# Scores of two pairs of heads per turn of TensorE, and products with v in two parts

## The chip, the cores and the metric

One NeuronCore of a Trainium2 chip runs the whole program in one launch. The metric is the device time of one execution in microseconds (us). The engines are TensorE (PE, with its weight loads as PEld), VectorE (DVE), ScalarE (ACT), GpSimd (POOL) and SyncE (SP, which mostly issues DMAs).

## The reference

Talking-heads attention over 4 batches, 12 heads, 448 positions and 64 columns, then two feed-forward parts. Only the attention is touched by the change:

```python
scores = scale * np.matmul(q, k.transpose(0, 1, 3, 2))
scores = np.einsum('bhij,hg->bgij', scores, w_pre)       # heads mixed before the softmax
scores = scores - np.max(scores, axis=-1, keepdims=True)
attn = np.exp(scores)
attn = attn / (np.sum(attn, axis=-1, keepdims=True) + 1e-09)
attn = np.einsum('bhij,hg->bgij', attn, w_post)          # and after it
x = np.matmul(attn, v)                                   # [4, 12, 448, 64] -> [1792, 768]
```

Behind it stand `h = x @ w_in; x = (h * cos(h)) @ w_out` and a soft mixture of 8 experts with `phi`, `w1` and `w2`. All data are float32; `w_in` and `w_out` come as 64-bit floats and are narrowed by the kernel.

## The kernel before

The program has three stages. `phase_a` is the attention, `phase_b` the first feed-forward part, `phase_c` the experts. `phase_b` begins when the attention ends (`start_b` is called by `phase_a` as `start_next` ahead of its last products), and reads `xT_d`, which the attention writes to DRAM.

`phase_a` works on 16 query tiles (4 for each batch, of 120 rows, or 90 in the short one), and on 60 groups of 30 mixed rows within them (4 groups a tile, 3 in the short one). For a tile:

- `q_prep` (L310) turns q by TensorE (tile `qt`) and splits it into two parts, `q_hi` and `q_lo`. `k_prep` (L287) does the same for k once a batch (`kt`, six of them).
- `scores` (L347) multiplies one pair of heads at a time: six matmuls, three for each head, on 64 rows of the array each, the two heads side by side in the upper and lower half (tiles `s`; such a run is called a score episode). Two copies take the results out of PSUM to `ss` (ACT or DVE), and a DMA from POOL sorts each head into `s2`, so that heads stand beside rows.
- `pre` (L395): for each group three matmuls with the mixing matrix (`pre`), a maximum on DVE (`mz`, L409), an exponential on ACT (`e`, L413). `fin` (L423) makes the group's weights `wc` on DVE.
- `post` (L437): four results for each group (`po`, three matmuls each), copied to `am`.
- `av` (L486): the products with v, in three parts of four heads. Each head uses 64 columns of the array (tiles `av`, L468); a copy takes each part to `xst`, and a DMA stores the tile.

Beside this, 64 pieces of `w_in` and `w_out` are narrowed (`narrow`, L506) on DVE, ACT and POOL.

None of this is issued as it is written. Each step is an `Op` with the engines that may do it and an assumed duration, with what it depends on, the buffers it takes and a due time in units of groups. `Plan.schedule` (L115) goes through time with these durations, takes for each engine the op that can start first and is due earliest, and so writes one fixed order for every engine. A change between ops marked `half` (scores and products) and all others adds `TURN` to an op, and `STAY` to its due time. Due times follow from constants: scores of a tile are due `S_DUE` groups ahead of its first group, spread over `S_SPAN`; k is turned `K_DUE` ahead of its scores; a group's `pre` is due `P_DUE` ahead, the products `AV_DUE` behind a tile's last group, spread over `AV_SPAN`.

PSUM has eight banks: three for `pre`, two for `po`, three (`ps`) for `s`, `kt`, `qt` and `av`. The first 24 users of `ps` take turns over all eight by the list `SPARE`. SBUF has eight `ss` buffers, two `s2`, one `xst`.

Of the kernel before, what the change touches and what calls it, by code (L numbers as in the profile page):

```python
# [56 lines left out]
class Slot:  # L57


    def __init__(self, tag):  # L60
        self.tag, self.users = tag, []


class Op:


    def __init__(self, ways, emit, deps, due, takes, moves, behind, half, late):
        self.ways, self.emit, self.due, self.half, self.late = ways, emit, due, half, late
        self.deps, self.takes, self.moves, self.behind = list(deps), list(takes), moves, list(behind)
        self.end = None  # L70


class Plan:
# [10 lines left out]
    def op(self, ways, emit, deps=(), due=0.0, takes=(), uses=(), moves=0.0, behind=(), half=False, late=0.0):  # L84


        o = Op(ways, emit, deps, due, takes, moves, behind, half, late)
# [27 lines left out]
    def schedule(self):  # L115
# [3 lines left out]
        after, halves = {}, False  # L119
# [4 lines left out]
        while ready:  # L124
            best = None
            starts = []
            for o in ready:
                r = self.room(o.takes)
                if r is None:
                    continue  # L130
                for e, dur in o.ways:
                    t = max([free[e], r] + [d.seen + (self.HOP if d.eng != e else 0.0) for d in o.deps]
                            + [d.start for d in o.behind])
                    if e == "PE" and o.half != halves:
                        dur += self.TURN
                    starts.append((t, t + dur, o, e, dur))
# [7 lines left out]
            for x in starts:  # L144
                t, end, o, e, dur = x
                if t <= first[e] + 0.05:
                    due = o.due + (STAY if e == "PE" and o.half != halves else 0.0)
                    if e not in pick or due < pick[e][0]:
                        pick[e] = (due, x)
# [10 lines left out]
            if e == "PE":  # L160
                halves = o.half
# [18 lines left out]
def phase_a(tc, ident, q, k, v, w_pre, w_post, xT_d, wide, start_next):  # L180
# [8 lines left out]
    with ExitStack() as ctx:  # L189
# [157 lines left out]
        def scores(ti, p, due):  # L347

            b, t = tiles[ti]
            n = ROWS[t]  # L350
            s = [Slot("ps") for _ in range(2)]
            x = {}

            def mul(e):
                pts = made["s", ti, p] = [bank(s[o], f"s{ti}_{2 * p + o}") for o in range(2)]
                for i, (x, y) in enumerate(((qh, kp), (qh, kr), (ql, kp))):
                    for o in range(2):
                        r = slice(64 * o, 64 * o + 64)
                        nc.tensor.matmul(pts[o][:n, :S], x[r, p, :n], y[r, p, :],  # L359
                                         start=(i == 0), stop=(i == 2))  # L360

            def out(o):
                def f(e):
                    if ti:
                        x[o] = room(sg, "ssrc", [120, S], F32, f"ss{ti}_{2 * p + o}")
                    else:

                        c = S * (2 * p + o)
                        x[o] = am[1].rearrange("p h t i -> p (h t i)")[:, c:c + S]
                    copy(e, x[o][:n], made["s", ti, p][o][:n, :S])  # L370
                return f

            def sort(o):
                h = 2 * p + o

                def f(e):
                    if h == 0:
                        s2t[ti] = room(sg, "s2", [120, 12, S], F32, f"s2_{ti}")
                    QUEUE[e].dma_start(out=s2t[ti][h::12, :n // 10], in_=x[o][:n])  # L379
                return f  # L380
            qk[ti, p] = plan.op([("PE", 0.8)], mul, [kdone[b, p], qdone[ti, p // 2]], due, takes=s, half=True)
            for o in range(2):
                h = 2 * p + o
                ss = [Slot("ssrc")] if ti else []
                if h == 0:
                    s2l[ti] = Slot("s2")
                c = plan.op(EV, out(o), [qk[ti, p]], due, takes=ss, uses=[s[o]])
                sorted_[ti, h] = plan.op([("POOL", 0.62)] if ti else [("SP", 1.0), ("POOL", 0.8)], sort(o), [c], due,
                                         takes=[] if h else [s2l[ti]], uses=ss + ([s2l[ti]] if h else []),
                                         moves=1.0 * n / 120, behind=[sorted_[ti, 0]] if h else [])  # L390
# [46 lines left out]
        def post(gi, jt, f, due):  # L437
# [10 lines left out]
            def out(e):  # L448
# [4 lines left out]
                                     [m] + ([avs[ti - 2, s] for s in range(3)] if ti > 1 else [sorted_[0, h] for h in range(H)] if ti else []), due, uses=[b])  # L453


        xst, xl = {}, {}

        def av_mul(ti, s, pt):
# [5 lines left out]
            for x in range(2):  # L464
                for jt in range(NJ):
                    for o in range(2):
                        g = 4 * s + 2 * x + o
                        nc.tensor.matmul(pt[64 * o:64 * o + 64, x * 120:x * 120 + n], vt[:, g, jt, :],  # L468
                                         am[ti % 2][:, g, jt, :n], start=(jt == 0), stop=(jt == NJ - 1))

        def av_out(ti, s, by):
            n = 30 * NG[tiles[ti][1]]
            copy(by, xst[ti][:, 2 * s:2 * s + 2, :n],
                 made["av", ti, s][:, :240].rearrange("p (x i) -> p x i", i=120)[:, :, :n])
# [11 lines left out]
        def av(ti, due):  # L486
# [4 lines left out]
            for s in range(3):  # L491
                d, sl_ = due + s / 3 * AV_SPAN, Slot("ps")
                avs[ti, s] = plan.op([("PE", 1.64)],
                                     lambda e, s=s, sl_=sl_: av_mul(ti, s, bank(sl_, f"av{ti}_{s}")),
                                     need + [vload[b, s]], d, takes=[sl_] + ([] if s else [xl[ti]]),
                                     uses=[xl[ti]] if s else [], behind=[avs[ti, 0]] if s else [], half=True)
                outs.append(plan.op([("ACT", 0.28), ("DVE", 0.36)], lambda e, s=s: av_out(ti, s, e),
# [59 lines left out]
        for b in range(B):  # L557
            for ti in range(4 * b, 4 * b + 4):
                g0, n = first[ti], NG[tiles[ti][1]]
                mark = [qk[ti - 1, 0]] if ti > 2 else [qk[1, 5]] if ti > 1 else [qk[0, 2]] if ti else []  # L560
                for p in range(6):
# [11 lines left out]
                    scores(ti, p, d)  # L573
# [19 lines left out]
        for s in range(3):  # L593
# [3 lines left out]
            av_out(NT - 1, s, "DVE" if s == 1 else "ACT")  # L597
# [669 lines left out]
```

## Time and profile before

| what | us |
|---|---|
| median of 3 runs (lowest, highest) | 911.07 (908.5, 912.84) |
| the profiled execution | 906.24 |
| its span, first to last instruction | 904.4 |
| TensorE busy in the span | 860.0 (95%) |
| VectorE, ScalarE, GpSimd busy | 627.5, 513.8, 178.9 |
| first matmul of `phase_b` | 498.24 |

A row of the trace has an instruction's start and length in us. Matmuls are pipelined, so that rows that follow each other overlap; what an instruction costs the engine is the distance from its start to the next start. A row with a count holds several equal instructions. A float32 matmul that isn't split by the kernel leaves two records (`po` x6 is one result of three matmuls, `pre` x2 one matmul, `av` x32 sixteen). Idle time stands behind a row in brackets with what ended it.

### The profile page before, as it was taken

Reading aid. Unit: us, or ns where it says so; the run is one execution under the profiler, and the core shown is the slowest. Engines: PE = TensorE matmul, PEld = TensorE weight load, DVE = VectorE, ACT = ScalarE, POOL = GpSimd, SP = SyncE. Lnnn points to the kernel's source line nnn. Section 1 sums busy time; section 2 is a strip of 40 time slices with the busy share of each in tenths; the row PEclk is TensorE's granted clock in tenths of the full one; section 3 lists DMA queues with packets and bytes.
Section 4 is the critical chain, followed back from the end, with each engine's and each line's share of the span. In section 5 each row is a group of like instructions: output and inputs, shape, how many; then the busy total and the mean of one; then the engine's idle time right before and its main releaser. Section 6 shows DMA issues by size and latency. Waiting matters only on the chain.

```text
span 904.4 us, 17763 instructions
## 1 busy us (share of the span) xinstructions
PE 860.0 (95%) x6636; PEld 605.2 (67%) x6636; DVE 627.5 (69%) x1286; ACT 513.8 (57%) x1134; POOL 178.9 (20%) x272
## 2 busy tenths in 40 slices
PE   7899999999999999999999799999999999989765
PEld 5467777776777777777778577776777787843212
DVE  4478878778779788788754687877877778843003
ACT  4477777677767777767655344555546457612003
POOL 2233443333434334334310000000000000010000
PEclk9999999999999999999999999999999999999778
DMA  7999897999788997979518892363464348899998
GB/s 166 202 197 232 221 241 207 221 209 270 215 211 223 237 233 174 253 211 236 155 32 225 224 212 73 120 215 135 158 226 141 122 153 273 298 339 411 418 401 307
DMA packets 181793, 198.91 MB, mean 220 GB/s; under 512 B 73600, under 2 KB 155458, under 8 KB 181708
## 3 DMA queue, kind: packets, MB, share of 16 engines
q1 hardware_dynamic: 164824, 159.18, 60.2%
q0 software_dynamic: 14272, 37.96, 18.7%
q8 instruction: 52, 0.85, 0.4%
q10 hardware_dynamic: 2612, 0.65, 0.4%
q14 instruction: 33, 0.27, 0.1%
HBM read 135.40 MB, written 23.59 MB: 176 GB/s over the span
## 4 chain that ended last, share of the span: by engine, by line
PE 83%; DMA 9%; DVE 2%; SPq 2%; ACT 2%; issue 1%; POOL 0%; DVEq 0%; ACTq 0%; POOLq 0%
PE po L444 17%; PE pre L406 15%; PE h L698 9%; PE av L468 8%; PE h L699 8%; PE h L701 8%; PE s L359 8%; DMA knat<-in_k_dram 2%; DMA ring<-in_moe_w_dram 2%; PE p L810 2%; DMA cg<-in_moe_w_dram 2%; PE eh L1061 2%; PE lg L749 1%; DMA s<-ss 1%; SPq L968 1%
## 5 line engine op out<-in xcount | busy, mean ns | idle before, releaser
L444 PEld LDWEIGHTS po<-wc,e 120*112 120x112 f32 x1440 | 171.6, 178 | 56.8 <-issue 42.5
L444 PE MATMUL po<-wc,e 120*112 120x120 f32 x1440 | 183.8, 270 | 0.5 <-ACT am L229 0.5
L406 PE MATMUL pre<-s,kron_pre 120*120 120x448 f32 x360 | 166.3, 551 | 3.8 <-ACT e L413 3.8
L379 POOL DMA_DIRECT2D s<-ss x180 | 107.0, 596 | 173.9 <-ACT ss L229 124.4
L409 DVE TENSOR_REDUCE mz<-pre 120x1 f32<-120x448 f32 x180 | 111.1, 621 | 42.4 <-PE pre L406 41.1
L698 PE MATMUL h<-x,wh 128*128 128x512 f32 (+1 forms) x384 | 140.0, 374 | 0.1
L699 PE MATMUL h<-x,wh 128*128 128x512 f32 (+1 forms) x384 | 136.6, 365 | 0.0
L413 ACT ACTIVATE e<-pre,mz 120x448 f32<-120x448 f32 x180 | 114.7, 638 | 25.2 <-DVE mz L409 22.7
L229 ACT COPY am<-po 112x360 f32<-112x360 f32 x190 | 87.6, 462 | 66.2 <-PE po L444 64.2
L698 PEld LDWEIGHTS h<-x,wh 128*128 128x128 f32 x384 | 72.4, 188 | 28.4 <-ACT cg L712 11.7
L701 PE MATMUL h<-x,wf 128*128 128x512 f32 (+1 forms) x384 | 87.7, 364 | 0.0
L712 ACT ACTIVATE cg<-h 128x512 int32<-128x512 f32 (+1 forms) x64 | 34.7, 541 | 90.8 <-PE h L701 88.3
L543 POOL TENSOR_TENSOR nar<-nar,cvt 128x384 uint32<-128x384 uint32 x64 | 64.2, 1003 | 98.4 <-DVE cvt L534 43.7
L468 PE MATMUL av<-am,v 112*64 112x120 f32 (+1 forms) x1536 | 83.0, 262 | 0.0
L468 PEld LDWEIGHTS av<-am,v 112*64 112x64 f32 x1536 | 74.0, 137 | 10.4 <-issue 5.5
L699 PEld LDWEIGHTS h<-x,wh 128*128 128x128 f32 x384 | 72.5, 189 | 11.3
L701 PEld LDWEIGHTS h<-x,wf 128*128 128x128 f32 x384 | 66.5, 188 | 11.9
L713 DVE SCALAR_TENSOR_TENSOR cg<-h,cg 128x512 f32<-128x512 f32 (+1 forms) x64 | 39.8, 622 | 48.4 <-ACT cg L712 48.4
L229 ACT COPY ss<-s 120x448 f32<-120x448 f32 (+1 forms) x104 | 54.1, 533 | 27.6 <-PE s L359 15.4
L1035 POOL MEMSET own<- 128x192 f32 x2 | 0.4, 253 | 345.3 <-PE si L1021 345.3
L651 DVE TENSOR_TENSOR wf<-wf,wh 128x768 fp32r<-128x768 f32 x64 | 60.9, 951 | 8.7 <-ACT wh L650 8.7
L406 PEld LDWEIGHTS pre<-s,kron_pre 120*120 120x120 f32 x360 | 53.2, 184 | 20.4 <-issue 11.7
(171 smaller groups left out, 1204.5 us busy)
## 6 DMA issues: line engine op xcount, KB each, us to landing
s<-ss POOLq DMA_DIRECT2D x144, 210.0 KB, 7.9
early<-in_moe_w_dram SPq DMA_DIRECT2D x36, 768.0 KB
wf<-w SPq DMA_DIRECT2D x64, 384.0 KB
raw<-in_moe_w_in_dram SPq DMA_DIRECT2D x32, 384.0 KB
w<-nar SPq DMA_DIRECT2D x64, 192.0 KB
raw<-in_moe_w_out_dram SPq DMA_DIRECT2D x32, 384.0 KB
gn<-in_moe_w_dram SPq DMA_DIRECT2D x16, 768.0 KB
early<-w SPq DMA_DIRECT2D x16, 384.0 KB
```

Source lines behind the costliest of these rows:

```text
L229: nc.scalar.copy(out=out, in_=in_)
L359: nc.tensor.matmul(pts[o][:n, :S], x[r, p, :n], y[r, p, :], start=(i == 0), stop=(i == 2))
L379: QUEUE[e].dma_start(out=s2t[ti][h::12, :n // 10], in_=x[o][:n])
L406: nc.tensor.matmul(prt[gi, c][:, :S], kpre, s2t[ti][:, 3 * g + c, :], start=True, stop=True)
L409: nc.vector.tensor_reduce(out=mz[gi][:, 0, c:c + 1], in_=prt[gi, c][:, :S], axis=AX.X, op=ALU.max, negate=True)
L413: nc.scalar.activation(out=et[gi][:, c, :], in_=prt.pop((gi, c))[:, :S], func=AF.Exp, bias=mz[gi][:, 0, c:c + 1], accum_out=mz[gi][:, 1, c ...
L444: nc.tensor.matmul(pt[:, :360].rearrange("p (g i) -> p g i", i=30)[:, :, 10 * c:10 * c + 10], et[gi][:, c, jt * CJ:(jt + 1) * CJ], wct[gi] ...
L468: nc.tensor.matmul(pt[64 * o:64 * o + 64, x * 120:x * 120 + n], vt[:, g, jt, :], am[ti % 2][:, g, jt, :n], start=(jt == 0), stop=(jt == NJ ...
L543: nc.gpsimd.tensor_tensor(out=f, in0=f, in1=x["t"], op=ALU.add)
L698: nc.tensor.matmul(pt, wh[:, c], xh[:, c, :], start=(c == 0), stop=False)
L699: nc.tensor.matmul(pt, wh[:, c], xl[:, c, :], start=False, stop=False)
L701: nc.tensor.matmul(pt, wl[:, c], xh[:, c, :], start=False, stop=(c == 5))
```

## The change

From the third tile on, `scores` takes two pairs of heads at once: twelve matmuls in one op, four `ps` banks, the four copies and DMAs as before. `av` has two parts (`AVP`) of six heads instead of three of four. The plan's mark `half` becomes a `mode`, "rows" for scores and "cols" for products, so that `TURN` and `STAY` also count between these two. The banks become two for `pre` and four for `ps`; `SPARE`, due times and assumed durations change. What is computed stays the same.

```diff
-PLACES = {"pre": 3, "post": 2, "ps": 3, "knat": 2, "qnat": 2, "ssrc": 8, "s2": 2, "e": 3, "wc": 2, "xst": 1,
+PLACES = {"pre": 2, "post": 2, "ps": 4, "knat": 2, "qnat": 2, "ssrc": 8, "s2": 2, "e": 3, "wc": 2, "xst": 1,
...
-SPARE = 3 * ["ps", "pre", "ps", "pre", "ps", "post", "pre", "post"]
-K_DUE, S_DUE, S_SPAN, P_DUE, AV_DUE, AV_SPAN, STAY = 4.0, 3.2, 3.6, 1.8, 0.7, 3.0, 0.4
+SPARE = 3 * ["ps", "pre", "ps", "post", "ps", "pre", "ps", "post"]
+K_DUE, S_DUE, S_SPAN, P_DUE, AV_DUE, AV_SPAN, STAY = 5.6, 4.8, 1.9, 1.9, 0.0, 1.0, 0.6
...
+PAIRED, AVP = 2, 2
...
-                    if e == "PE" and o.half != halves:
+                    if e == "PE" and o.mode != mode:
                         dur += self.TURN
...
-                              deps=[avs[4 * b - 1, c]] if b else [], behind=behind)
+                              deps=[avs[4 * b - 1, s] for s in range(AVP)] if b else [], behind=behind)
...
-        def scores(ti, p, due):
+        def scores(ti, pairs, due):
...
-            s = [Slot("ps") for _ in range(2)]
+            s = {(p, o): Slot("ps") for p in pairs for o in range(2)}
...
+                for p in pairs:
+                    pts = made["s", ti, p] = [bank(s[p, o], f"s{ti}_{2 * p + o}") for o in range(2)]
+                    for i, (x, y) in enumerate(((qh, kp), (qh, kr), (ql, kp))):
+                        for o in range(2):
+                            r = slice(64 * o, 64 * o + 64)
+                            nc.tensor.matmul(pts[o][:n, :S], x[r, p, :n], y[r, p, :],
+                                             start=(i == 0), stop=(i == 2))
...
-            qk[ti, p] = plan.op([("PE", 0.8)], mul, [kdone[b, p], qdone[ti, p // 2]], due, takes=s, half=True)
+            m = plan.op([("PE", 0.09 + 0.6 * len(pairs))], mul,
+                        [kdone[b, p] for p in pairs] + [qdone[ti, p // 2] for p in pairs], due,
+                        takes=list(s.values()), mode="rows")
...
+        XS = 6 // AVP
...
-            for x in range(2):
+            for x in range(XS):
                 for jt in range(NJ):
                     for o in range(2):
-                        g = 4 * s + 2 * x + o
+                        g = 2 * (XS * s + x) + o
...
-            for s in range(3):
-                d, sl_ = due + s / 3 * AV_SPAN, Slot("ps")
-                avs[ti, s] = plan.op([("PE", 1.64)],
+            for s in range(AVP):
+                d, sl_ = due + s / AVP * AV_SPAN, Slot("ps")
+                avs[ti, s] = plan.op([("PE", 0.05 + 0.77 * XS)],
...
-                    scores(ti, p, d)
+                    if ti < PAIRED:
+                        scores(ti, [p], d)
+                    elif p % 2:
+                        scores(ti, [p - 1, p], d)
```

What it does to the order of TensorE's instructions, at three places. In the names the first number is the tile or group, the second the head, part or pair, the last a buffer's.

TensorE, fourth tile (`s3`), the scores of the first heads. Before:

```order
L359 MATMUL s3_0_772<-k_hi_104,q_lo_108 120x448
L359 MATMUL s3_1_773<-k_hi_104,q_lo_108 120x448
L468 MATMUL av0_1_784<-am0_109,v_106 64x90 x16
L359 MATMUL s3_2_815<-k_hi_104,q_hi_107 120x448
L359 MATMUL s3_3_816<-k_hi_104,q_hi_107 120x448
L359 MATMUL s3_2_815<-k_lo_105,q_hi_107 120x448
L359 MATMUL s3_3_816<-k_lo_105,q_hi_107 120x448
L359 MATMUL s3_2_815<-k_hi_104,q_lo_108 120x448
L359 MATMUL s3_3_816<-k_hi_104,q_lo_108 120x448
L293 MATMUL kt1_0_831<-ident_62,knat1_0_516 128x112 x4
L444 MATMUL po4_3_840<-wc4_660,e4_566 112x12x10 x3
L406 MATMUL pre6_2_848<-s2_1_297,kron_pre_96 120x448
```

and with the change:

```order
L361 MATMUL s3_0_842<-k_hi_104,q_lo_108 120x448
L361 MATMUL s3_1_843<-k_hi_104,q_lo_108 120x448
L361 MATMUL s3_2_850<-k_hi_104,q_hi_107 120x448
L361 MATMUL s3_3_851<-k_hi_104,q_hi_107 120x448
L361 MATMUL s3_2_850<-k_lo_105,q_hi_107 120x448
L361 MATMUL s3_3_851<-k_lo_105,q_hi_107 120x448
L361 MATMUL s3_2_850<-k_hi_104,q_lo_108 120x448
L361 MATMUL s3_3_851<-k_hi_104,q_lo_108 120x448
L449 MATMUL po5_2_869<-wc5_798,e5_663 112x12x10 x3
L294 MATMUL kt1_0_882<-ident_62,knat1_0_501 128x112 x4
L294 MATMUL kt1_1_890<-ident_62,knat1_0_501 128x112 x4
L330 MATMUL qt3_2_903<-ident_62,qnat3_506 128x120 x2
```

Scores of heads 2 and 3 follow those of 0 and 1 at once, where a part of the products stood between; one `po` is then ahead of the two turns of k (`kt`) that use the next `ps` banks.

TensorE, products of the first tile (`av0`) with v. Before, the first of three parts, between scores:

```order
L359 MATMUL s2_8_644<-k_hi_104,q_lo_108 120x448
L359 MATMUL s2_9_645<-k_hi_104,q_lo_108 120x448
L468 MATMUL av0_0_664<-am0_109,v_106 64x90 x16
L359 MATMUL s2_10_691<-k_hi_104,q_hi_107 120x448
L359 MATMUL s2_11_692<-k_hi_104,q_hi_107 120x448
```

and with the change both parts:

```order
L449 MATMUL po3_2_682<-wc3_587,e3_508 112x12x10 x3
L475 MATMUL av0_0_690<-am0_109,v_106 64x90 x24
L475 MATMUL av0_1_727<-am0_109,v_106 64x90 x24
L449 MATMUL po3_3_761<-wc3_587,e3_508 112x12x10 x3
L411 MATMUL pre5_2_766<-s2_1_297,kron_pre_96 120x448
```

The two parts stand in one piece between two `po`, no longer beside scores.

TensorE, the end of the stage: the last `pre` (`pre59_2`), the last `po` and the products of the last two tiles. Before:

```order
L406 MATMUL pre59_2_5742<-s2_15_5304,kron_pre_96 120x448
L444 MATMUL po58_0_5746<-wc58_5728,e58_5679 112x12x10 x3
L444 MATMUL po58_1_5751<-wc58_5728,e58_5679 112x12x10 x3
L444 MATMUL po58_2_5757<-wc58_5728,e58_5679 112x12x10 x3
L444 MATMUL po58_3_5762<-wc58_5728,e58_5679 112x12x10 x3
L468 MATMUL av14_0_5771<-am0_109,v_106 64x120 x16
L468 MATMUL av14_1_5790<-am0_109,v_106 64x120 x16
L444 MATMUL po59_0_5808<-wc59_5766,e59_5713 112x12x10 x3
L444 MATMUL po59_1_5813<-wc59_5766,e59_5713 112x12x10 x3
L444 MATMUL po59_2_5818<-wc59_5766,e59_5713 112x12x10 x3
L444 MATMUL po59_3_5823<-wc59_5766,e59_5713 112x12x10 x3
L468 MATMUL av14_2_5828<-am0_109,v_106 64x120 x16
```

and with the change:

```order
L449 MATMUL po57_3_5763<-wc57_5660,e57_5609 112x12x10 x3
L411 MATMUL pre59_2_5768<-s2_15_5338,kron_pre_96 120x448
L449 MATMUL po58_0_5771<-wc58_5698,e58_5647 112x12x10 x3
L449 MATMUL po58_1_5776<-wc58_5698,e58_5647 112x12x10 x3
L449 MATMUL po58_2_5782<-wc58_5698,e58_5647 112x12x10 x3
L449 MATMUL po58_3_5787<-wc58_5698,e58_5647 112x12x10 x3
L449 MATMUL po59_0_5797<-wc59_5791,e59_5685 112x12x10 x3
L449 MATMUL po59_1_5801<-wc59_5791,e59_5685 112x12x10 x3
L449 MATMUL po59_2_5806<-wc59_5791,e59_5685 112x12x10 x3
L449 MATMUL po59_3_5811<-wc59_5791,e59_5685 112x12x10 x3
L475 MATMUL av15_0_5871<-am1_110,v_106 64x90 x24
L475 MATMUL av15_1_5899<-am1_110,v_106 64x90 x24
```

The products of the tile before the last (`av14`) stand ahead of these rows now, and `po59` follows `po58` without products between.

## Rows read from the trace of the kernel before

**Rows 1.** Busy time by engine, 45 to 452 us: stretch, length, engines, clock, DMA share, GB/s

```profile
45.00:452.00 407.00, 405.55 (x3449) 297.18 (x3449) 329.11 (x727) 291.87 (x744) 160.92 (x228) 1.00 0.92 219
```

**Rows 2.** TensorE in order of time, 59 to 66 us: start, length, engine, line, what, count

```profile
59.75 0.78 PE L444 MATMUL po<-wc,e 120*112 120x120 f32 x6
60.45 0.47 PE L359 MATMUL s<-k_hi,q_hi 64*120 64x448 f32 x2
60.76 0.37 PE L359 MATMUL s<-k_lo,q_hi 64*120 64x448 f32 x2
60.96 0.37 PE L359 MATMUL s<-k_hi,q_lo 64*120 64x448 f32 x2
61.26 1.46 PE L468 MATMUL av<-am,v 112*64 112x90 f32 x32
...
63.16 0.37 PE L359 MATMUL s<-k_hi,q_lo 64*120 64x448 f32 x2
63.46 0.87 PE L444 MATMUL po<-wc,e 120*112 120x120 f32 x6
64.17 0.92 PE L406 MATMUL pre<-s,kron_pre 120*120 120x448 f32 x2
64.92 0.78 PE L444 MATMUL po<-wc,e 120*112 120x120 f32 x6
65.54 0.92 PE L406 MATMUL pre<-s,kron_pre 120*120 120x448 f32 x2
```

**Rows 3.** The same view, first tile, two score episodes back to back

```profile
16.89 0.37 PE L359 MATMUL s<-k_hi,q_hi 64*90 64x448 f32 x2
17.10 0.37 PE L359 MATMUL s<-k_lo,q_hi 64*90 64x448 f32 x2
```

**Rows 4.** The same view, products with v: one episode, then two in a row

```profile
445.26 1.86 PE L468 MATMUL av<-am,v 112*64 112x120 f32 x32
447.06 0.45 PE L359 MATMUL s<-k_hi,q_hi 64*90 64x448 f32 x2
...
486.46 3.50 PE L468 MATMUL av<-am,v 112*64 112x120 f32 x64
489.89 2.91 PE L444 MATMUL po<-wc,e 120*112 120x120 f32 x24
```

**Rows 5.** Costliest groups: line, engine, operation, count | busy, mean ns | idle before

```profile
L444 PE MATMUL po<-wc,e 120*112 120x120 f32 x1440 | 183.8, 270 | 0.5 <-ACT am L229 0.5
L406 PE MATMUL pre<-s,kron_pre 120*120 120x448 f32 x360 | 166.3, 551 | 3.8 <-ACT e L413 3.8
L409 DVE TENSOR_REDUCE mz<-pre 120x1 f32<-120x448 f32 x180 | 111.1, 621 | 42.4 <-PE pre L406 41.1
L413 ACT ACTIVATE e<-pre,mz 120x448 f32<-120x448 f32 x180 | 114.7, 638 | 25.2 <-DVE mz L409 22.7
L229 ACT COPY ss<-s 120x448 f32<-120x448 f32 (+1 forms) x104 | 54.1, 533 | 27.6 <-PE s L359 15.4
```

**Rows 6.** In order of time, the end of the stage: TensorE, ScalarE, VectorE

```profile
483.64 2.89 PE L444 MATMUL po<-wc,e 120*112 120x120 f32 x24
484.81 0.64 ACT L413 ACTIVATE e<-pre,mz 120x448 f32<-120x448 f32 x1
485.99 0.53 DVE L431 TENSOR_TENSOR wc<-kron_post,mz 120x360 f32<-120x360 f32 x1
498.24 0.50 PE L698 MATMUL h<-x,wh 128*128 128x512 f32 x1
511.78 1.71 PE L677 MATMUL pw<-early,gn 128*32 128x512 f32 x8 [5.07 <-DMA gn<-in_moe_phi_dram]
```

**Rows 7.** In order of time, the start of the stage; then busy times, 35 to 40 us

```profile
36.45 0.53 ACT L229 COPY ss<-s 120x448 f32<-120x448 f32 x1 [0.88 <-DMA s<-ss]
37.66 1.85 PE L406 MATMUL pre<-s,kron_pre 120*120 120x448 f32 x2 [1.03 <-ACT e L413]
35.00:40.00 5.00, 3.35 (x8) 1.77 (x9) 2.41 (x6) 2.96 (x9) 1.16 (x2) 0.76 1.09 205
```

More of the change, by code (lines that the diff above doesn't have):

```diff
@@ L64, with __init__ @@
 class Op:
-    def __init__(self, ways, emit, deps, due, takes, moves, behind, half, late):
-        self.ways, self.emit, self.due, self.half, self.late = ways, emit, due, half, late
+    def __init__(self, ways, emit, deps, due, takes, moves, behind, mode, late):
+        self.ways, self.emit, self.due, self.mode, self.late = ways, emit, due, mode, late
         self.deps, self.takes, self.moves, self.behind = list(deps), list(takes), moves, list(behind)
@@ L82, in __init__, with op @@
         self.ops, self.order, self.held = [], [], {t: [] for t in places}
-    def op(self, ways, emit, deps=(), due=0.0, takes=(), uses=(), moves=0.0, behind=(), half=False, late=0.0):
-        o = Op(ways, emit, deps, due, takes, moves, behind, half, late)
+    def op(self, ways, emit, deps=(), due=0.0, takes=(), uses=(), moves=0.0, behind=(), mode="", late=0.0):
+        o = Op(ways, emit, deps, due, takes, moves, behind, mode, late)
         for s in list(takes) + list(uses):
@@ L146, in schedule @@
                 if t <= first[e] + 0.05:
-                    due = o.due + (STAY if e == "PE" and o.half != halves else 0.0)
+                    due = o.due + (STAY if e == "PE" and o.mode != mode else 0.0)
                     if e not in pick or due < pick[e][0]:
@@ L160, in schedule @@
             if e == "PE":
-                halves = o.half
+                mode = o.mode
             o.end = end
@@ L378, in f @@
                         s2t[ti] = room(sg, "s2", [120, 12, S], F32, f"s2_{ti}")
-                    QUEUE[e].dma_start(out=s2t[ti][h::12, :n // 10], in_=x[o][:n])
+                    QUEUE[e].dma_start(out=s2t[ti][h::12, :n // 10], in_=x[h][:n])
                 return f
-            qk[ti, p] = plan.op([("PE", 0.8)], mul, [kdone[b, p], qdone[ti, p // 2]], due, takes=s, half=True)
[L382 to L390, printed above, removed]
+            m = plan.op([("PE", 0.09 + 0.6 * len(pairs))], mul,
+                        [kdone[b, p] for p in pairs] + [qdone[ti, p // 2] for p in pairs], due,
+                        takes=list(s.values()), mode="rows")
+            for p in pairs:
+                qk[ti, p] = m
+                for o in range(2):
+                    h = 2 * p + o
+                    ss = [Slot("ssrc")] if ti else []
+                    if h == 0:
+                        s2l[ti] = Slot("s2")
+                    c = plan.op(EV, out(p, o), [m], due, takes=ss, uses=[s[p, o]])
+                    sorted_[ti, h] = plan.op([("POOL", 0.62)] if ti else [("SP", 1.0), ("POOL", 0.8)], sort(h), [c],
+                                             due, takes=[] if h else [s2l[ti]], uses=ss + ([s2l[ti]] if h else []),
+                                             moves=1.0 * n / 120, behind=[sorted_[ti, 0]] if h else [])
         el, et, mz, prt, wct, expd, wcl, mixed = {}, {}, {}, {}, {}, {}, {}, {}
@@ L591, in phase_a @@
         start_next()
-        for s in range(3):
+        for s in range(AVP):
             av_mul(NT - 1, s, ps.tile([128, 512], F32, tag="ps", name=f"av{NT - 1}_{s}"))
```

36 lines of the change are left out of this document (15 added, 21 removed).

## Prediction

> **What bounds the kernel now.** I read the busy times of the attention stage first, then TensorE's instructions in order of time there, then what VectorE and ScalarE do between two of them. Between 45 and 452 us TensorE is busy for 405.55 of 407.00 us at a granted clock of 1.00, 2.4 GHz [rows 1]: there is next to nothing in that stretch that it waits for, so the stage is as long as the sum of what its instructions take, start to start. VectorE has 329.11 us and ScalarE 291.87 us of work in the same time [rows 1], 81% and 72%; the DMA engines are busy to 92%. So time is only won by making TensorE's stream itself shorter, and only kept as long as no wait comes in.
>
> The stream holds three shapes of the array: the score matmuls (64 rows, two heads side by side, "rows"), the products with v (64 columns, "cols") and all the rest ("full"). [rows 2] show what a change of shape costs. Six records of po take 0.62 us start to start when a pre follows (64.92 to 65.54), but 0.70 when scores follow (59.75 to 60.45): the first scores start 0.08 late. The first pair of scores then holds the engine for 0.31 us (60.45 to 60.76), the second for 0.20 (60.76 to 60.96): 0.11 more. On the way out the last pair takes 0.30 (63.16 to 63.46) and not 0.20, and the six po behind it 0.71 (63.46 to 64.17) and not 0.62. So each turn costs about 0.19 us, half ahead of it and half in the first instruction behind it. From scores to products with v it is the same at the front (60.96 to 61.26, 0.30). Where no turn lies between, this is gone: in the first tile two score episodes stand back to back, and the first pair of the second takes 0.21 (16.89 to 17.10) [rows 3]. The same for the products: one episode alone takes 1.80 us (445.26 to 447.06), two in a row 3.43 (486.46 to 489.89), 0.17 less than two alone [rows 4], and that is only the part that lies between them.
>
> **The change, part by part.** *Fewer turns.* The matmuls are the same ones, in number and shape; only their order differs. I counted the changes of shape in the two orders of TensorE, from the first matmul to the last product with v. Before: 64 full to rows, 67 back, 22 rows to cols, 25 cols to rows, 19 full to cols, 15 back, 212 in all. After: 46, 46, none, none, 16 and 15, 123 in all. 89 turns go. A turn is between 0.15 us (into the products, whose first matmul is short) and 0.20 us; at 0.175 that is 89 x 0.175 = 15.6 us, from 13.4 to 17.8. As TensorE has no idle time to give it back to [rows 1], all of it comes off the stage, and what stands behind the stage moves up with it.
>
> *One bank less for pre (3 to 2).* Each pre needs its bank back from the pre two ahead of it, and so VectorE's maximum and ScalarE's exponential of that one: 0.62 and 0.64 us [rows 5]. In an undisturbed place TensorE left a pre at 483.64 and its exponential, started at 484.81, ended 0.64 us later at 485.45: 1.8 us [rows 6]. Adding up plain start-to-start times from [rows 2] (pre 0.75, po 0.62, a score episode 0.6 plus its turns), the new order leaves at least 2.0 us nearly everywhere: the tight pattern is pre, po, pre, po, pre, which gives 0.62 + 0.75 + 0.62 = 1.99. 22 of some 165 places have less than 2.2 us, 28 less than 2.4. With a chain of 1.8 us nothing waits; with one copy of 0.53 or 0.6 us in its way each time (2.4 us) the sum of the shortfalls is 7.6 us. Before, with three banks, most places had over 4 us. Ends 0 and 7.6; I take 1.5, near the low end, because a copy stands in the way only in some places and po, with its two banks and an equally tight 0.62 us between uses, shows 0.5 us of idle in all of the page's 1440 records [rows 5].
>
> *Scores of four heads at once.* They take all four ps banks, and the next user of ps must wait for copies: two on ScalarE at 0.53 us [rows 5], two on VectorE, 1.3 to 1.5 us if nothing is ahead of them. In the order 20 places leave under 2 us between a bank's scores and its next user, most of them k transposes in the last tile of a batch (the first place shown with the change: the other half of the scores and one po, then k transposes). One more copy ahead of each costs up to 0.6 us x 20 = 12; nothing waits if the copies come first. Ends 0 and 12; I take 1.5, by the same row of po. Other users of ps come later, and pre and po go on meanwhile.
>
> *Products in two parts of six heads.* 48 episodes become 32 of the same matmuls; their turns are in the count. The copies out go from three of 240 columns to two of 360, one instruction less for each tile, on engines that are not the bound: nothing. The load of v waits for both parts of the last tile of a batch instead of for its own part; the order leaves 19 us until the next products, before 11 to 14: nothing.
>
> *The start.* Until 41 us TensorE waits for ScalarE, whose copies of the second tile's scores wait for buffers: the last of them starts at 36.45, and pre waits behind it until 37.66, at a granted clock of 0.76 over 35 to 40 us, partly the lower of its levels, 1.2 GHz [rows 7]. The change leaves these tiles unpaired and the same copies in ScalarE's way, but with two banks TensorE stands one pre further back when they end: 0.75 us, twice that at the lower clock. Ends 0 and 3; I take 1.5.
>
> *The end of the stage.* The last group's weights depend on the last pre: VectorE starts them at 485.99 for 0.53 us [rows 6]. In the new order the same four po cover that, but the eight products ahead are gone, so the last products follow the last po at once and wait for its copy (0.5 us). The loads of w_out queue on SP behind those weights; they start some 4 us nearer to the next stage, whose wait for phi (5.07 us at 511.78 [rows 6]) could grow. Ends 0 and 4; I take 0.5.
>
> Sum: -15.6 + 1.5 + 1.5 + 1.5 + 0.5 = -10.6 us. The profiled execution took 906.24 us, so 895.6. It lies 4.8 us under the median of the runs, 911.07; I carry the difference over: **900.5 us**, 1.2% faster.
>
> A rule speaks against this. The Trainium skill, TensorEngine Tiling (Array Packing), section PSUM Bottleneck, says that tiling speeds up TensorE but not the evacuation of PSUM, which may then become the bottleneck. By the rows VectorE would be busy for 329 us of some 394, 84%, which bounds nothing on average; by the rule the time goes to the first rival's.
>
> **The rivals.** *Evacuation takes the gain back.* VectorE and ScalarE are strictly in order, and four copies at once push maxima and exponentials back. If each tight place sees one copy in its way, pre costs 7.6, ps some 5, the start 1.5 and the end 1: 15.1 against 15.6, and the time is 910.5, no change. For it: 81% on VectorE and fewer banks. Against: before, TensorE waited 0.5 us in 1440 po and 3.8 us in 360 pre, all of that at the start [rows 5, 7]. This is the mechanism that the page describes. Chance 0.14.
>
> *Slower: two banks set the pace.* If the chain from pre to the end of the exponential takes 2.7 us (two copies in the way), 48 places fall short by 17.9 us together; with 7.5 for ps, start and end that is +9.8, 921 us. It decides from about 2.55 us, where the shortfalls alone are 12 us. The 1.8 us above speak against it. Chance 0.05.
>
> *A turn is worth only its front half.* If the slower first instruction stays (its weights loaded late for another reason), 89 x 0.09 = 8.0 us go, less the 5.0 of waits: 908. Against it is the 0.21 us pair [rows 3], which has no turn ahead of it and is not slow. Chance 0.06.
>
> **How the numbers follow.** Forecast 0.75; it spans 893 (turns at 17.8, no waits) to 906. The range goes from 893 to 908: it takes in the forecast and the third rival, and leaves out the slower rival, most of the first and a little below. Under 0.5% (4.6 us) a measurement here can't tell a change from none. Faster by more: nearly all of the forecast and about a third of the first and third rivals, 0.80. Within: 0.15. Slower: 0.05.
>
> **What would show it.** Right: TensorE's first pair of scores at 0.31 us once in twelve records and not in six, 46 score episodes, the stage's last product some 10 us earlier (now 498.24 is the next stage's first matmul [rows 6]), everything behind shifted and equally long. The bank terms show as idle time ahead of pre (released by e) and ahead of k transposes and scores (released by ss copies): 1.5 us each. Wrong: over 8 us of such idle time, k or s waiting for DMA, or a phi wait well over 5 us.

## The result, and the profile after

| | before | changed | ratio (95% interval) |
|---|---|---|---|
| first comparison, 5 runs each | 911.85 (908.50 to 914.99) | **903.49** (902.36 to 904.71) | 0.9902 (0.9877 to 0.9928) |
| again, beside other kernels, 6 runs (before: 23) | 913.31 | 902.35 (899.05 to 905.12) | 0.9887 (0.9838 to 0.9936) |
| a third time, 6 runs (before: 23) | 911.64 | 899.48 (898.48 to 906.41) | 0.9897 (0.9853 to 0.9940) |

The changed kernel is faster by 1.0 to 1.1%. The forecast was 900.5, the range 893 to 908. The three profiled executions took 903.49, 899.31 and 898.48 us; below they are *after*, *again* and *third*.

**The turns are gone, at the price read.** TensorE of the changed kernel, in order of time, in the place of [rows 2]:

```profile
58.34 0.92 PE L411 MATMUL pre<-s,kron_pre 120*120 120x448 f32 x2
59.19 0.47 PE L361 MATMUL s<-k_hi,q_hi 64*120 64x448 f32 x2
59.49 0.36 PE L361 MATMUL s<-k_lo,q_hi 64*120 64x448 f32 x2
59.70 0.37 PE L361 MATMUL s<-k_hi,q_lo 64*120 64x448 f32 x2
59.90 0.36 PE L361 MATMUL s<-k_hi,q_hi 64*120 64x448 f32 x2
60.10 0.36 PE L361 MATMUL s<-k_lo,q_hi 64*120 64x448 f32 x2
60.30 0.37 PE L361 MATMUL s<-k_hi,q_lo 64*120 64x448 f32 x2
60.60 0.87 PE L449 MATMUL po<-wc,e 120*112 120x120 f32 x6
61.31 0.92 PE L411 MATMUL pre<-s,kron_pre 120*120 120x448 f32 x2
```

The first pair of scores still holds the engine for 0.30 us (59.19 to 59.49). The pair at 59.90, where the second pair of heads begins, takes 0.20; in the kernel before, a turn stood there.

Busy times from the start to the first matmul of `phase_b`, before and after (TensorE's is the first number behind the length):

```profile
0.00:498.24 498.24, 486.28 (x4131) 357.00 (x4131) 371.77 (x818) 341.23 (x860) 175.30 (x257) 1.00 0.88 208
```

```profile
0.00:488.71 488.71, 473.14 (x4131) 360.86 (x4131) 367.10 (x811) 338.10 (x852) 174.23 (x257) 1.00 0.90 209
```

TensorE is busy for 13.1 us less (13.5 and 13.4 in *again* and *third*), 0.15 us for each of the 89 turns, and idle for 3.6 us more. The difference of the two is the stage's gain.

The page's groups, the first three with their counterparts in [rows 5]:

```profile
L449 PE MATMUL po<-wc,e 120*112 120x120 f32 x1440 | 183.6, 269 | 1.1 <-ACT am L230 0.9
L411 PE MATMUL pre<-s,kron_pre 120*120 120x448 f32 x360 | 169.2, 557 | 7.3 <-issue 4.5
L230 ACT COPY ss<-s 120x448 f32<-120x448 f32 (+1 forms) x114 | 55.7, 538 | 8.5 <-DMA s<-ss 5.8
```

The idle time ahead of `pre` went from 3.8 to 7.3 us, 4.5 of it one wait at the start, and its mean from 551 to 557 ns. `po` waits for 1.1 us and not 0.5. ScalarE's copies `ss` now have less to wait for from TensorE: what ends their idle time is the sort of an earlier tile (5.8 us), which holds the buffer.

**The start.** The wait of [rows 7] has shrunk, and another has come behind it:

```profile
47.32 3.02 PE L411 MATMUL pre<-s,kron_pre 120*120 120x448 f32 x4 [4.49 <-issue]
```

```profile
45.00:50.00 5.00, 2.68 (x4) 1.23 (x5) 0.62 (x1) 0.40 (x1) 0.62 (x2) 0.76 1.21 212
```

This `pre` needs the last sorted scores of the second tile. GpSimd had issued the last of those sorts by 33.45 us, and it landed some 14 us later, with the DMA engines at 1.21. The row names no releaser; in *again* the same wait is put down to the sort:

```profile
46.93 1.82 PE L411 MATMUL pre<-s,kron_pre 120*120 120x448 f32 x2 [3.27 <-DMA s<-ss]
```

A clock partly at 1.2 GHz follows, as before.

**The end of the stage.** In order of time, SyncE, ScalarE and TensorE, as in [rows 6]:

```profile
481.19 0.53 DVE L436 TENSOR_TENSOR wc<-kron_post,mz 120x360 f32<-120x360 f32 x1
481.80 1.92 SPq L674 DMA_DIRECT2D early<-w  x4
484.94 0.39 ACTq L488 DMA_DIRECT2D xT_d<-xst  x1
488.71 0.50 PE L709 MATMUL h<-x,wh 128*128 128x512 f32 x1
495.20 0.39 ACT L230 COPY xst<-av 128x270 f32<-128x270 f32 x1 [5.65 <-DMA xT_d<-xst]
495.38 8.89 SPq L869 DMA_DIRECT2D gn<-in_moe_phi_dram  x4
505.87 1.94 PE L688 MATMUL pw<-early,gn 128*32 128x512 f32 x8 [8.71 <-DMA gn<-in_moe_phi_dram]
```

The next stage's first matmul comes at 488.71 and no longer at 498.24. The wait for phi has grown from 5.07 to 8.71 us. The weights `wc`, behind which SyncE's loads of w_out stand, end at 481.7, 7 us ahead of that first matmul; before they ended 11.7 us ahead of it (486.52, [rows 6]). The store of the last tile but one, issued at 484.94, frees the only `xst` at 495.20, and SyncE's loads of phi follow.

Where the time went, cut at instructions that all four profiles have (the first `wtr` is the first transpose of weights behind the wait for phi):

| us | before | after | again | third |
|---|---|---|---|---|
| start to the first matmul of `phase_b` | 498.24 | 488.71 | 488.55 | 487.83 |
| from there to the first `wtr` | 20.78 | 25.62 | 23.47 | 24.06 |
| from there to the last `h` | 269.86 | 272.52 | 269.76 | 269.79 |
| from there to the end | 115.54 | 114.40 | 115.30 | 114.55 |

The attention won 9.5 to 10.4 us, and 2.7 to 4.8 went again at the boundary. The extra 2.7 us of *after* in the third row are a clock at 1.2 GHz from 747.3 to 754.2 us. *Third*, whose order and whose wait ahead are the same, does not have it. For each, the wait, then busy times from 745 to 752 us (the clock is the third number from the end, 0.67 and 1.00):

```profile
746.26 1.13 PE L774 MATMUL lgsum<-gn,st 128*128 128x512 f32 x2 [1.87 <-DVE gn L768]
```

```profile
745.00:752.00 7.00, 5.74 (x25) 5.26 (x26) 4.60 (x13) 3.28 (x6) 0.00 (x0) 0.67 0.96 342
```

```profile
743.87 1.12 PE L774 MATMUL lgsum<-gn,st 128*128 128x512 f32 x2 [1.87 <-DVE gn L768]
```

```profile
745.00:752.00 7.00, 6.98 (x59) 6.77 (x59) 4.26 (x13) 5.10 (x10) 0.00 (x0) 1.00 0.98 350
```

### The profile page after: what moved, and what is told of

Its sections match the earlier page's. It is cut to its first block, busy times and chain, and to the rows that moved or that the text cites. A ratio compares the mean times of both kernels' runs of the same rounds, so it can differ in the third digit from the quotient of the medians.

```text
span 901.3 us, 17759 instructions
## 1 busy us (share of the span) xinstructions
PE 848.5 (94%) x6636; PEld 611.7 (68%) x6636; DVE 622.7 (69%) x1279; ACT 510.2 (57%) x1125; POOL 177.8 (20%) x272
## 4 chain that ended last, share of the span: by engine, by line
PE 76%; DMA 14%; DVE 4%; issue 2%; SPq 1%; ACT 1%; POOL 1%; POOLq 0%; ACTq 0%; DVEq 0%
PE po L449 14%; PE pre L411 13%; PE h L709 9%; PE h L710 8%; PE h L712 8%; PE av L475 8%; PE s L361 6%; DMA s<-ss 5%; DMA early<-in_moe_w_dram 2%; PE p L821 2%; DMA ring<-in_moe_w_dram 2%; DMA cg<-in_moe_w_dram 2%; PE eh L1072 2%; PE lg L760 1%; SPq L979 1%
## 5 line engine op out<-in xcount | busy, mean ns | idle before, releaser
L411 PE MATMUL pre<-s,kron_pre 120*120 120x448 f32 x360 | 169.2, 557 | 7.3 <-issue 4.5
L709 PE MATMUL h<-x,wh 128*128 128x512 f32 (+1 forms) x384 | 142.3, 379 | 0.0
L710 PE MATMUL h<-x,wh 128*128 128x512 f32 (+1 forms) x384 | 138.7, 370 | 0.0
L230 ACT COPY am<-po 112x360 f32<-112x360 f32 x183 | 84.5, 462 | 52.2 <-PE po L449 50.4
L709 PEld LDWEIGHTS h<-x,wh 128*128 128x128 f32 x384 | 74.2, 193 | 28.2 <-ACT cg L723 10.9
L710 PEld LDWEIGHTS h<-x,wh 128*128 128x128 f32 x384 | 74.2, 193 | 11.3
L475 PE MATMUL av<-am,v 112*64 112x120 f32 (+1 forms) x1536 | 77.6, 261 | 0.0
```

The lines of the kernel that those rows point to most:

```text
L230: nc.scalar.copy(out=out, in_=in_)
L411: nc.tensor.matmul(prt[gi, c][:, :S], kpre, s2t[ti][:, 3 * g + c, :], start=True, stop=True)
L709: nc.tensor.matmul(pt, wh[:, c], xh[:, c, :], start=(c == 0), stop=False)
L710: nc.tensor.matmul(pt, wh[:, c], xl[:, c, :], start=False, stop=False)
```

## The experiments

The kernels that vary the changed one stand against the kernel before on their own chip, so that ratios can be compared. TensorE's idle time is that from 52 us to the first matmul of `phase_b`, the length of that stretch less the busy time in it.

| kernel | turns | us | ratio to before (95%) | first matmul of `phase_b` | idle |
|---|---|---|---|---|---|
| before | 212 | 911.07 | 1 | 498.24 | 1.45 |
| changed: after, again, third | 123 | above | 0.9902, 0.9887, 0.9897 | 488.71, 488.55, 487.83 | 2.38, 2.65, 2.14 |
| e1_turns | 197 | 915.13 | 1.0053 (1.0027 to 1.0079) | 510.19 | 12.06 |
| e2_unpaired | 153 | 911.25 | 0.9980 (0.9941 to 1.0018) | 497.76 | 4.63 |
| e3_parts3 | 123 | 908.50 | 0.9965 (0.9929 to 1.0000) | 493.66 | 6.74 |
| e3_again | 123 | 906.74 | 0.9965 (0.9933 to 0.9997) | 492.17 | 6.37 |
| e4_banks | 183 | 912.51 | 0.9998 (0.9967 to 1.0029) | 503.86 | 7.24 |
| e5_vlate | 123 | 908.21 | 0.9986 (0.9954 to 1.0018) | 494.25 | 8.79 |
| e6_phi | 123 | 900.25 | 0.9861 (0.9809 to 0.9913) | 490.36 | 2.67 |
| e7_before_phi | 212 | 909.41 | 0.9950 (0.9915 to 0.9985) | 504.08 | 6.72 |
| e9_phi_xst | 123 | 899.46 | 0.9882 (0.9843 to 0.9921) | 489.88 | 5.80 |
| e10_all | 125 | 903.30 | 0.9927 (0.9897 to 0.9957) | 493.30 | 6.83 |

The idle time of one profile is not the order's alone. In this stage e9_phi_xst has the order of e6_phi on every engine, and 5.80 us of idle time against 2.67; 2.35 us of it is one wait of `po`, behind a piece of `w_in` that ScalarE had to wait for. TensorE and ScalarE of e9_phi_xst:

```profile
74.37 1.48 PE L449 MATMUL po<-wc,e 120*112 120x120 f32 x12 [2.35 <-ACT am L230]
```

```profile
73.42 0.56 ACT L547 ACTIVATE nar<-raw 128x384 f32<-128x384 uint32 x1 [3.57 <-DMA raw<-in_moe_w_in_dram]
```

Nor does an edit of one constant change one thing: the planner writes a new order for VectorE and ScalarE too in e1 to e5 and in e10_all.

### Are the turns what was won?

**e1_turns**: the changed kernel with six products parts, no extra due time for a turn.

```diff
-..., AV_SPAN, STAY = ..., 1.0, 0.6
+..., AV_SPAN, STAY = ..., 3.0, 0.0
-PAIRED, AVP = 2, 2
+PAIRED, AVP = 2, 6
```

> The changed kernel with more turns and nothing else: products in six parts, spread over three groups, and no bonus in the plan for staying in a shape. Same matmuls, same 46 score episodes; the product episodes go from 16 to 53, the turns from 123 to 197. Theory (a turn costs both halves, 0.15 us into the products and 0.19 out): 37 x 0.34 = 12.5 us slower than the changed kernel, about 916. Rival (only the late start of 0.09 counts): 74 x 0.09 = 6.7 us, about 910. Third (turns are hidden by waits anyway): no change, 903.

Busy times of e1_turns from the start to the first matmul of `phase_b`, then its longest wait:

```profile
0.00:510.19 510.19, 486.59 (x4131) 361.04 (x4131) 386.59 (x856) 342.18 (x879) 175.19 (x257) 0.99 0.87 206
```

```profile
507.59 2.67 PE L475 MATMUL av<-am,v 112*64 112x90 f32 x32 [6.44 <-ACT xst L230]
```

74 turns more, and TensorE is busy for 13.45 us more than in *after* (486.59 less 473.14). A clock partly at 1.2 GHz is in both, here on the last products (2.67 us; sixteen such products take 1.46 in [rows 2]), in *after* at 47 us, and is worth under 1 us in the difference. That is 0.18 us for each turn, where the half price of the third rival would give 0.09. The other 8.0 us by which the stage is longer are waits, 6.44 us of it one on `xst` at the last of the small parts. Of the whole 21.5 us, 6 to 10 came back behind the stage (against the three profiles of the changed kernel), so that the time fits the expected 916 us is in part luck; the price of a turn is read from the busy time.

**e2_unpaired**: the changed kernel with every tile's scores one pair at a time.

```diff
-PAIRED, AVP = 2, 2
+PAIRED, AVP = 99, 2
```

> The changed kernel with single pairs of heads everywhere; banks, due times and products as in the change. In the order, 153 turns instead of 123 (63 score episodes instead of 46). Theory: 30 turns x 0.19 = 5.7 us slower than the changed kernel, less what four banks at once cost (up to 1.5), so 4 to 6: about 908. Rival (the pairs' demand for four banks eats what they save): within 1.5 us of the changed kernel, 903 to 905.

30 turns of the 89 are the pairing's own, 5.3 us at the price of the sum; the other 59 come from the marks, the due times and the banks. By the ratios the pairing is worth 0.8 to 0.9%, 7 to 8 us. In the profile, from the start to the first matmul of `phase_b`, TensorE is busy for 9.1 us more than in *after* (482.23 against 473.14) and idle as long (15.5 and 15.6 us). Some 3 us of the 9.1 are a lower clock, 0.92 in place of 0.96 from 10 to 52 us and 0.89 from 70 to 85 us, there behind a late piece of `w_in` as in e9_phi_xst; nearly 6 are left, 0.19 us for a turn.

### What the products in two parts do

**e3_parts3** and **e3_again**, the same kernel on two chips, the second beside *third*:

```diff
-PAIRED, AVP = 2, 2
+PAIRED, AVP = 2, 3
```

> The changed kernel with the products in three parts of four heads as before; everything else as in the change. The plan puts the three parts in a row, so that the turns stay at 123. Theory (parts cost only by their turns): the same time, 903.5 within 1.5 us; one copy more for each tile lies on engines that are not the bound. Rival (two parts are worth something themselves, by fewer copies or banks): 2 us or more slower.

> The changed kernel with the products in three parts of four heads instead of two of six: 123 turns as in the changed kernel, the same matmuls. The prediction gave the parts nothing; by that it takes what the changed kernel takes, within 2 us. Rival: a third part needs one more of the four ps banks and one more copy out for each tile, and VectorE and ScalarE, which are waited for in order, have that copy in the way of am and of the exponential; then it is 3 to 6 us slower than the changed kernel on the same chip.

The prediction gave the two parts nothing. With three, TensorE's order has the same 123 turns, its busy time in the stage is the same (*third*, then e3_again), and yet the stage is 4.34 us longer:

```profile
52.00:487.83 435.83, 433.69 (x3908) 334.87 (x3907) 340.72 (x757) 312.61 (x795) 160.50 (x228) 1.00 0.90 213
```

```profile
52.00:492.17 440.17, 433.80 (x3906) 334.35 (x3904) 344.03 (x760) 313.19 (x805) 160.37 (x228) 1.00 0.87 210
```

Nearly all of it is idle time (6.37 us against 2.14), in few places. TensorE of e3_again, four with a wait that *third* does not have, or has shorter:

```profile
196.87 0.87 PE L449 MATMUL po<-wc,e 120*112 120x120 f32 x6 [0.55 <-ACT am L230]
...
218.89 1.35 PE L475 MATMUL av<-am,v 112*64 112x120 f32 x22 [1.37 <-DVE q_lo L339]
...
268.68 0.64 PE L411 MATMUL pre<-s,kron_pre 120*120 120x448 f32 x1 [0.71 <-ACT e L418]
...
392.61 0.56 PE L449 MATMUL po<-wc,e 120*112 120x120 f32 x3 [0.75 <-DVE am L228]
```

The products at 218.89 wait for VectorE's split of q, which gives back a bank of `ps`; the two `po` and the `pre` wait for copies `am` and an exponential. The same four waits, equal within 0.01 us, stand in e3_parts3, so they belong to the order and not to one execution. That the third part's bank or copy causes them is not shown. Ahead of the two `po` and the `pre`, the engine that they wait for has no copy of the products in the last 5 us; ahead of the last one VectorE has a step of narrowing that took 2.34 us, where the same step takes 0.36 in most places:

```profile
388.65 2.34 DVE L539 TENSOR_SCALAR cvt<-cvt 128x384 uint32<-128x384 uint32 x1
```

So two parts in place of three, with the order that the planner makes of them, are worth 4.3 us of stage, and in the time 6 to 7 us (0.9965 against 0.9897). Of the part beyond the stage e3_again has 2.8 us behind the boundary (272.62 between the first `wtr` and the last `h`, *third* 269.79), where it shows the lower clock that *after* shows too.

### The banks alone

**e4_banks**: the kernel before with the new banks.

```diff
-PLACES = {"pre": 3, "post": 2, "ps": 3, ...
+PLACES = {"pre": 2, "post": 2, "ps": 4, ...
```

> The kernel before with two banks for pre and four for ps and nothing else; the planner's order has 183 turns then (before 212, changed kernel 123). Theory: 29 turns less at 0.16 us, -4.6, and 1 to 4 us of new waits ahead of pre and at the start: 906 to 911 us, within 0.5% of before. Rival (the two banks set the pace): idle time ahead of pre, released by the exponential, of over 8 us, and 914 us or more.

29 turns fewer and no gain. At the price of the sum they give 4 to 5 us, but TensorE's busy time from the start is only 1.0 us less (485.26 against 486.28; under 3 with the lower clock from 10 to 52 us, 0.92 against 0.96, taken out), and its idle time is longer (7.24 us from 52 us on, 1.45 in the profile of before). So the new banks bring nothing without the rest, and the number of turns alone did not tell the time. How much of those waits is the banks' can't be told from it: 1.62 us is a turn of k at 92.49 us that waits for its load, and e7_before_phi shows below that the order of before has such waits too in some executions.

### The start

**e5_vlate**: the changed kernel; the first batch's v loaded from ScalarE's queue, behind the second tile's scores.

```diff
-            vload[b, c] = dma(0.55, 1.9, start, ...
+            vload[b, c] = plan.op([("SP" if b else "ACT", 0.55)], start, moves=1.9, ...
...
+        for c in range(3):
+            vload[0, c].behind = [mixed[4]]
```

> The changed kernel with the first load of v (1.3 MB) issued from ScalarE's queue some 15 us later instead of from SP at 23.5 us. Theory (TensorE's wait of 4.49 us at 47.3 us is for the second tile's sorted scores, whose transfers queue in the DMA engines behind v): the wait goes to under 1 us and the lower clock behind it too, 4 to 6 us faster than the changed kernel, 898. Rival (the sorts are late for another reason, such as k and the weights' first loads, or the copies behind them): less than 1.5 us of change.

The wait at the start fell from 4.49 us (3.27 in *again*) to 1.82, as it should if the sorts stood behind v. But the stage then idles for 8.79 us in place of 2.4, and the ratio, 0.9986, is 0.8 to 1% above the changed kernel's, not 4 to 6 us below it. The later waits are not for v: the longest, 1.85 us at 364.29, is a `po` that waits for a copy on VectorE. As the order of VectorE and ScalarE changed with the edit, it doesn't tell what the load of v costs where it stood. That the wait at the start hangs on the transfers ahead is borne out; that it costs what it lasts is not.

### The boundary

**e6_phi** loads phi early into a tile of its own; **e7_before_phi** is the same edit on the kernel before.

```diff
+        ph = sp.tile([128, 6, 32], F32, name="ph")
...
+        for a in range(4):
+            nc.sync.dma_start(out=ph[32 * a:32 * a + 32], in_=phi[192 * a:...
         load_wo(0)
...
-        ws, ph = gn_all[:, 7168:7680], gn_all[:, 7680:7872].rearrange(...
-        for a in range(4):
-            nc.sync.dma_start(out=ph[32 * a:32 * a + 32], in_=phi[192 * a:...
+        ws = gn_all[:, 7168:7680]
```

> The changed kernel with phi loaded early into a tile of its own, so that the first matmul pw of the next stage no longer waits for four transfers which SyncE starts only after the store of the last transposed tile. Theory: the wait ahead of pw (8.71 us in the changed kernel) is a tail of the stage's transposes and stores and not of the stage's matmuls; with phi out of it most of the wait and of the lower clock behind it goes, 5 to 10 us, to 892 to 899 us. Rival: the wait passes to the next thing that hangs on the same store (ScalarE's copy of ws into gn_all, or the load of w_out), and less than 4 us come back.

> The same edit of phi on the kernel before. Its wait is 5.07 us with a lower clock behind it, so the theory expects 4 to 7 us less than before, 905 to 907 us; and between this kernel and e6_phi the change without its cost at the boundary, -10 to -13 us. If the boundary is not where the change gave time back, e6_phi and e7_before_phi stand as far apart as the changed kernel and the kernel before, some 8 us.

In e6_phi the wait for phi is gone, and another stands 20 us later. TensorE, then ScalarE:

```profile
498.77 1.07 PE L688 MATMUL pw<-early,ph 128*32 128x512 f32 x8
...
518.95 0.79 PE L709 MATMUL h<-x,wh 128*128 128x512 f32 x1 [5.23 <-ACT wh L661]
```

```profile
496.55 0.39 ACT L230 COPY xst<-av 128x270 f32<-128x270 f32 x1 [5.34 <-DMA xT_d<-xst]
...
518.06 0.83 ACT L661 CAST wh<-wf 128x768 fp32r<-128x768 f32 x1 [7.79 <-DMA wf<-w]
```

TensorE waits at 518.95 for the split weights `wh`, ScalarE for their load, and SyncE issued that load behind the second `x`, for which it waited 8.4 us until the last tile's store had landed. So the rival was right: the tail behind the last `wc` is one of loads and stores, phi was only the first to show it, and 2.1 us come back (0.9861 against 0.9887, whose intervals overlap). On the kernel before the same edit gives 3.9 us, 0.9950, and the wait for `wh` that takes its place is shorter, 2.01 us at 534.54: there the loads had started 11.7 us ahead of the first matmul and not 7. Between e6_phi and e7_before_phi lie 9.2 us on one chip (900.25 and 909.41), which is about what lies between the changed kernel and the one before, and less than the 10 to 13 expected: that phi out of the way brings back what the change lost at the boundary is not borne out.

**e9_phi_xst** and **e10_all** were to give `xst` a second buffer, e10_all with v late as well.

```diff
-..., "wc": 2, "xst": 1,
+..., "wc": 2, "xst": 2,
```

> The kernel with phi loaded early, and with two buffers for the transposed tile xst instead of one; the planner's order is unchanged, 123 turns. With phi early alone, ScalarE's first copy of the last xst waited 5.34 us for the store of the tile ahead, SyncE's load of the second x for the last store another 8.4 us, and TensorE 5.23 us at 518.95 for weights that queue behind that load. Theory: the one buffer is what is late at the stage's end; with two the last copies, the store and the loads behind it come some 5 us earlier, TensorE's wait goes, and the time is 4 to 7 us under the changed kernel's. Rival: the transfers share the DMA engines with the loads of w_out, so the store lands as late as before, and there is no more gain than phi alone gave, 2 us.

> As the one with phi early and two xst, and the first batch's v loaded behind the second tile's scores, so that the sorts of the second tile do not stand behind 1.3 MB of v. In the first such trial TensorE's wait at the start fell from 4.49 to 1.82 us, with no clear gain in the time. Theory: -1 to -3 us against the kernel with phi early and two xst. Rival: what the start gains comes back as waits later in the stage, and the two take the same time.

The edit missed. The table only tells the planner; the tile itself is still taken from a pool with one buffer, as the wait shows, 5.25 us, with e6_phi's 5.34 above:

```profile
495.98 0.39 ACT L230 COPY xst<-av 128x270 f32<-128x270 f32 x1 [5.25 <-DMA xT_d<-xst]
```

The orders of all engines are those of e6_phi, so e9_phi_xst is e6_phi once more: 0.9882 beside *third*'s 0.9897. Over both pairs phi early is worth 0 to 2 us on the changed kernel, which these runs can't tell from nothing. Two `xst` were not tried. e10_all is then e6_phi with v late, at 0.9927, and again it is slower with v late (+3.8 us against e9_phi_xst on the same chip): no wait is left at 46 us, but one of 3.27 us stands at 95.22, behind ScalarE, which waited 7.75 us there for the store of the only `xst`. No kernel tried is surely faster than the changed one.

## Why the prediction was right, and where it was not

- **Turns, -15.6: right in kind, and near in size.** All 89 went, and TensorE's busy time in the stage fell by 13.1 to 13.5 us, 0.15 us a turn; by e1_turns a turn costs 0.18, by e2_unpaired some 0.19, where 0.175 was taken. The 13.1 us less the 3.6 us of new idle time are the stage's shift of 9.5 in *after*. The third rival (half price) falls. A turn has no fixed price, though: in e4_banks 29 fewer gave under 3 us. The Trainium skill, TensorEngine Tiling (Array Packing), Key Properties, says that a change of tiling mode drains TensorE; the rows agree that it costs time, at 0.30 us for a pair behind a change and 0.20 for one that is not.
- **The start, +1.5: near in size, wrong in mechanism.** TensorE's idle time between 10 and 52 us went from 5.26 to 7.3 to 7.6 us, +2.1 to 2.4. The step said that ScalarE's copies hold TensorE one `pre` further back. Those waits shrank; the time goes in waiting for sorts that land late behind other transfers, and the prediction had costed the start from the engines alone.
- **Two banks for `pre` and four heads at once, +3.0 together: right in kind, not separable.** Idle time in the stage grew by 0.7 to 1.2 us; the rows of `pre` grew by 2.9 us in all (169.2 against 166.3), the start's part included, which the busy time above already holds. That is some 1 to 4 us. The first rival (evacuation takes all) and the slower one (two banks set the pace, over 8 us ahead of `pre`) fall. The Trainium skill, TensorEngine Tiling (Array Packing), PSUM Bottleneck, which the prediction names for the first rival, says that after a fourfold speedup of TensorE the copies out of PSUM may become the bottleneck; here they showed as single waits of up to 1.2 us and not as a limit.
- **Products in two parts, "nothing": wrong.** By e3 they save 4.3 us of waits that the new order would have with three parts. The step counted instructions on engines that are not the bound; it counted neither the bank of `ps` that each part takes nor the order that the planner makes of three parts, and which of them costs is open. It did not show in the sum, because the bank terms had been priced without those waits.
- **The end of the stage, +0.5: mis-sized.** It measured +2.7 to +4.8 up to the first `wtr`, and the wait for phi, 8.0 to 8.7 us, is one of the prediction's own signs of being wrong. The mechanism was named (the loads of w_out queue behind the last weights and start nearer to the next stage, by 4.7 us), with 4 as its upper end; I took 0.5 because the four `po` cover the weights. That covers TensorE, not SyncE's queue, whose tail is what the next stage waits for.
- **The carry from the profile to the median, +4.8: wrong, and it made good the other error.** The sum gave 895.6 for a profiled execution; the three took 903.49, 899.31 and 898.48, 5.8 us less than before on average and not 10.6. The medians fell by 8.4, 11.0 and 12.2. The profiled execution of before lay 4.8 to 7 us under its medians, those of the changed kernel 0 to 3. e7_before_phi shows what can lie in this: its attention has the order of the kernel before on every engine (with the loads of phi besides on SyncE), and ends 5.84 us later (504.08). TensorE there, and busy times of that stretch with the clock at 0.72:

```profile
75.55 0.45 PE L293 MATMUL kt<-ident,knat 112*128 112x112 f32 x1 [4.28 <-DMA knat<-in_k_dram]
```

```profile
70.00:82.00 12.00, 7.72 (x54) 6.08 (x54) 5.77 (x13) 4.50 (x11) 4.29 (x6) 0.72 1.09 221
```

The last matmul of a turn of k waits 4.28 us for its load, and a lower clock follows; the profile of before has nothing there. e4_banks, with the due times of before, has such a wait of 1.62 us. In the changed order the first turns of the same k come later (78.26 us in *after*, 73.08 in before), and in its three profiles no `kt` waits for more than 0.3 us. That the change also saved time in such executions could close the gap of 4.8 us, but it is not shown, and e9_phi_xst has a wait of 2.35 us for another late load in the changed order. What the sum gave too much and what the carry added cancelled, so the closeness of 900.5 to the three medians is partly luck; for the change from median to median, 8.4 to 12.2 us, the -10.6 stands.

## What to carry to other kernels

Where an engine is busy for 99% of a stage, count what is lost between its instructions by kind of neighbour: turns of the array at 0.15 to 0.18 us were worth 1% here, and what is computed did not have to change. Where a planner writes the order, compare the orders before a time is put down to the constant that was edited. A stage's work made shorter does not move the transfers behind it: look what the queue of loads is released by, and how far ahead of the next stage that is, before and after. A count of buffers belongs into every step that changes how long or how often one is held, even where the instructions on both sides are free; and one profile is one execution, whose waits for transfers need not be the median's.

## What the runs showed of the hardware

The same wait of 1.87 us ahead of `lgsum` is followed by about 7 us at 1.2 GHz in *after* and not in *again*, *third* or before, which is worth 2.7 us in a kernel whose instructions are the same. The Trainium skill, TensorE: Matmul & The Clock Gate, Part 1, says that the number of matmuls which run at the lower clock at a kernel's start differs from run to run; these rows show such a difference in the middle of a kernel, behind a wait. A load that came late in one execution, and not in another of the same order, cost 4.28 us on a turn of k (e7_before_phi beside before) and 2.35 us on `po` behind a piece of `w_in` (e9_phi_xst beside e6_phi). Moving 1.3 MB of loads (e5_vlate, e10_all) shortened or ended a wait at 45 us, and both kernels were slower; as the order changed with the loads, what they cost where they stood stays open.
